# Half-sample fold, tables turned on TensorE, a given order on VectorE and ScalarE, and moved backward buffers in a spectral mixer with MLP

## Chip, cores, metric

One core of one Trainium2 chip. The metric is the device time of one execution in microseconds (us); a "run" is one execution, and a kernel's time is the median of its fast runs. A run more than 1.5% above the fastest of its kernel counts as slow; all comparisons below use the other, fast runs only, except where one slow run is shown as such. The granted clock is the share of its full clock that TensorE was given, as the profile reads it; "idle" is the time in which an engine is not busy.

## The reference

Sixteen-bit inputs and outputs, S = 2048 rows, D = 448 columns, F = 1792 hidden columns. The kernel computes the layer's output and the gradients of x, of the filter weights `w_r` and `w_i` (2048 x 225 each), and of the MLP's weights and biases.

```python
h  = x + irfft2(rfft2(layernorm(x)) * (w_r + 1j * w_i))      # over both axes
u  = gelu(einsum("bsd,sf->bdf", layernorm(h), w1) + b1)
h2 = h + transpose(einsum("bdf,fs->bds", u, w2) + b2)
# outputs: h2, and the vector-Jacobian product with grad_out for x, w_r, w_i, w1, b1, w2, b2
```

## The kernel before

The transforms are matmuls: a transform along the columns (tables `csF`), one along 16 row blocks (`Rm`), a re-sort through DMA, and a second transform (`Ut`, `Vt`), then the same backwards (`UTt`, `VTt`, `RTm`, `csI`). I call the stages: column transform, second transform, row inverse; the spectral part runs once forward (0 to about 138 us), then comes the MLP with the gradient of its hidden layer, then the spectral part again for the gradients. In between, "fill" matmuls of independent products (in the forward part the product of w2 and grad_out, later the gradients of w2 and w1) are put into TensorE's idle time by counts given by hand. The program's order is kept on TensorE and on the one DMA queue; VectorE and ScalarE are ordered by a scheduler.

```python
N_FILL_F = (50, 4, 16, 3, 16, 2)   # fill counts: ahead of the column transform, per tile in it,
                                   # ahead of the second transform, per step in it, after it, per row-inverse tile
tc.manual_schedule(engines={PE, SP})             # [arguments shortened]

def w_io(Wv, dr, di, store, eng):                # filter weights: 9 transfers for each of w_r, w_i
    for c_, d in ((0, dr), (1, di)):
        ...                                      # [cut] sb = Wv[part:P:8, g0:g1, c_, 0:DF]: rows of 225 numbers
        for f in range(4):
            go(f, 0, 16, ...); yield
            go(4 + f, g0, 16, ...); yield
        go(4, 0, 1, ...); yield

def w_mult(c2, xc, Wv, conj):                    # product with the weights: four VectorE operations,
    ...                                          # [cut] then one negation on ScalarE
    sc.activation(out=y[:, :, 2, :], in_=y[:, :, 0, :], func=ACT.Copy, scale=-1.0)

def bwd_mult(c2, xc):                            # in the loop of the backward second transform
    xs = Xs[:, 2 * c2:2 * c2 + 2, :, :]
    y = w_mult(c2, xc, W_view_B, True)
    ve.tensor_tensor(out=xs, in0=xs, in1=srow[...], op=ALU.mult)     # scale the stored coefficients
    ...                                          # [cut] four more VectorE operations: gradient of the weights

m448 = ring(r448, 0, 8, D)                       # eight row buffers
def load_xt(t):                                  # last stage: x comes back tile by tile
    xt = m448.next()
    nc.sync.dma_start(out=xt, in_=x_pt[:, t, :])
    xts.append(xt)
def gx_consumer(t, py):                          # five row buffers a tile: xt, gx, and three in ln_bwd
    xt = xts.pop(0)
    if t + 1 < NT: load_xt(t + 1)
    ...                                          # [cut] normalise, layer norm backward, store gx
```

## Time and profile before

Time before: 465.3 us (median of four runs, 464.8 to 469.7).

The head of the page of the kernel before: the span, each engine's busy time, the DMA packets, and the shares of the chain that ended last.

```profile
span 463.0 us, 6021 instructions
...
PE 370.3 (80%) x1920; PEld 187.3 (40%) x1920; DVE 261.9 (57%) x725; ACT 239.7 (52%) x485; POOL 51.8 (11%) x54
...
DMA packets 175144, 84.18 MB, mean 182 GB/s; under 512 B 123272, under 2 KB 170376, under 8 KB 174984
...
PE 44%; DVE 18%; DMA 18%; SPq 8%; ACT 6%; POOL 3%; issue 2%; DVEq 0%; ACTq 0%; POOLq 0%
```

No engine is busy throughout, so the time is made of waits between engines. Windows of the same kernel, for the forward part, the MLP, and the last two stretches of the backward part (the loop of the second transform with the weight product; then the row inverse, the gradient of w1 and the tail). Columns: window, its length, busy time of PE, PEld, DVE, ACT, POOL, then granted TensorE clock, DMA share, GB/s.

```profile
0.00:138.00 138.00, 95.83 (x506) 49.32 (x507) 105.13 (x330) 71.56 (x135) 48.77 (x50) 0.95 0.69 158
138.00:286.00 148.00, 136.18 (x723) 70.62 (x723) 87.27 (x226) 54.76 (x118) 2.73 (x3) 0.99 0.88 214
...
318.60:386.20 67.60, 56.38 (x262) 26.10 (x261) 30.72 (x64) 45.75 (x89) 0.00 (x0) 0.92 0.56 169
386.20:463.00 76.80, 55.31 (x313) 29.21 (x311) 35.22 (x97) 48.99 (x110) 0.00 (x0) 0.87 0.59 167
```

Read the first line so: TensorE works 95.8 of 138 us. TensorE's longest waits in the kernel before (sum, number of times, longest):

```profile
PE ps_ff L151 <- ACT rS L592: 15.1, 4, 8.6
PE ps_ff L151 <- DMA rX<-rX: 12.7, 6, 4.5
PE ps_mm L151 <- DMA rS<-in_B_w_dram: 10.0, 5, 3.0
...
PE ps_mm L151 <- DMA rst<-rE: 5.2, 1, 5.2
```

The first hides the weights: ScalarE's negation waits for VectorE's product, and that waits for the weight loads. The second is the transposes of x by DMA. And in the last stretch of the kernel before (386 us to the end), this is VectorE's largest wait by sum:

```profile
DVE r_80 L909 <- DMA out_dram<-r_80: 20.8, 14, 3.6
```

`r_80` is the ring of eight row buffers; VectorE waits for a store to free one.

### The profile page before, as it was taken

What the parts mean: (1) busy time and instruction counts of PE and PEld (TensorE: products, weight loads), DVE (VectorE), ACT (ScalarE), POOL (GpSimd) and SP (SyncE); (2) the same over time, 40 slices, a digit from 0 to 9 for tenths busy, and PEclk for the clock granted to TensorE, in tenths of its full rate; (3) what the DMA queues carried; (4) which work ended last, traced back from release to release, by engine and by line L of the source; (5) the groups of instructions that cost most, each with busy time, mean ns of one, the idle gap of its engine ahead of it and who ended that gap; (6) DMA issues with size and microseconds to landing.
All of it is one profiled execution on the core that took longest, in us unless ns stands there. A gap on an engine that the chain in (4) does not pass through costs nothing.

```text
span 463.0 us, 6021 instructions
## 1 busy us (share of the span) xinstructions
PE 370.3 (80%) x1920; PEld 187.3 (40%) x1920; DVE 261.9 (57%) x725; ACT 239.7 (52%) x485; POOL 51.8 (11%) x54
## 2 busy tenths in 40 slices
PE   2856577598979999788799999959389799898680
PEld 1323333244634545344355555424134355443340
DVE  9998952493892888621159777010186631443555
ACT  0646553375655564121223436735368677777671
POOL 6107996000000000000200000000000000000000
PEclk9989998799998999999999999988989899998885
DMA  8998897425325995699979995996645557667543
GB/s 254 238 205 154 172 148 179 110 80 144 119 121 162 328 303 129 148 280 227 289 145 228 181 207 89 197 225 200 170 154 175 159 164 215 177 163 196 160 149 130
DMA packets 175144, 84.18 MB, mean 182 GB/s; under 512 B 123272, under 2 KB 170376, under 8 KB 174984
## 3 DMA queue, kind: packets, MB, share of 16 engines
q1 hardware_dynamic: 175112, 83.80, 72.5%
q8 instruction: 15, 0.25, 0.2%
q14 instruction: 17, 0.14, 0.1%
HBM read 27.55 MB, written 22.04 MB: 107 GB/s over the span
## 4 chain that ended last, share of the span: by engine, by line
PE 44%; DVE 18%; DMA 18%; SPq 8%; ACT 6%; POOL 3%; issue 2%; DVEq 0%; ACTq 0%; POOLq 0%
PE ps_mm L151 36%; PE ps_ff L151 8%; SPq L489 5%; DMA out_dram<-r_80 5%; DMA r_80<-h_d 4%; DVE stats L644 3%; POOL Ut L403 2%; DVE r_80 L911 2%; DMA r_80<-in_A_x_dram 2%; DMA r_72<-in_B_w_dram 1%; DMA rst<-rE 1%; DMA rS<-in_B_w_dram 1%; DVE r_73 L298 1%; DMA rst<-rB 1%; DVE rB L682 1%
## 5 line engine op out<-in xcount | busy, mean ns | idle before, releaser
L151 PEld LDWEIGHTS <-rst 112*128 112x128 bf16 x480 | 47.4, 101 | 68.7 <-issue 11.4
L151 PE MATMUL ps_mm<-rC,rst 112*128 112x512 bf16 (+1 forms) x256 | 56.3, 367 | 10.9 <-DMA rst<-rB 8.7
L151 PE MATMUL ps_mm<-rG,rst 112*128 112x512 bf16 x224 | 55.1, 396 | 5.2 <-DMA rst<-rE 5.2
L151 PE MATMUL ps_mm<-rE,rS 128*128 128x448 bf16 x224 | 43.4, 353 | 10.0 <-DMA rS<-in_B_w_dram 10.0
L151 PE MATMUL ps_mm<-rB,r_72 128*128 128x448 bf16 x224 | 45.4, 362 | 3.4 <-DVE rB L757 2.2
L151 PE MATMUL ps_mm<-rC,rE 128*128 128x448 bf16 x144 | 37.7, 399 | 9.8 <-DMA rC<-in_grad_out_dram 8.9
L151 PEld LDWEIGHTS <-r_73 128*128 128x128 bf16 (+1 forms) x352 | 33.9, 111 | 27.6 <-issue 3.5
L151 PE MATMUL ps_mm<-rD,r_73 128*128 128x448 bf16 x224 | 43.3, 352 | 0.0
L151 PEld LDWEIGHTS <-rS 128*128 128x128 bf16 (+1 forms) x288 | 27.7, 98 | 35.3 <-DMA rS<-in_B_w_dram 12.2
L995 ACT CAST rO<-ps_mm 128x512 bf16<-128x512 f32 x56 | 32.4, 591 | 17.3 <-PE ps_mm L151 15.3
L1010 ACT CAST rO<-ps_mm 128x512 bf16<-128x512 f32 (+1 forms) x63 | 31.6, 536 | 6.0 <-PE ps_mm L151 4.7
L151 PEld LDWEIGHTS <-r_72 128*128 128x128 bf16 x224 | 22.3, 100 | 26.3 <-issue 6.5
L151 PE MATMUL ps_ff<-csI,rAT 113*128 113x448 bf16 x128 | 31.0, 367 | 1.8 <-ACT rAT L613 1.8
L865 DVE SCALAR_TENSOR_TENSOR r_80<-ps_mm,b2col,r_80 128x448 bf16<-128x448 f32 x16 | 10.8, 683 | 33.3 <-DMA r_80<-h_d 19.1
L872 ACT ACTIVATE r_80<-rC 128x448 bf16<-128x448 bf16 x16 | 9.2, 576 | 39.0 <-DMA out_dram<-r_80 35.7
L151 PEld LDWEIGHTS <-rE 128*128 128x128 bf16 x144 | 15.4, 107 | 29.6 <-issue 12.2
L905 ACT ACTIVATE r_80<-ps_mm 128x448 bf16<-128x448 f32 x16 | 8.7, 545 | 33.2 <-PE ps_mm L151 33.2
L151 PE MATMUL ps_ff<-rS,UTt 128*128 128x452 bf16 x32 | 12.1, 379 | 15.1 <-ACT rS L592 15.1
L613 ACT CAST rAT<-ps_ff 113x512 bf16<-113x512 f32 x32 | 18.5, 590 | 8.4 <-PE ps_ff L151 8.4
L906 DVE CUSTOM_DVE_ANT_0 r_80<-r_80 128x448 bf16<-128x448 bf16 x16 | 10.0, 624 | 22.6 <-ACT r_80 L905 15.4
L151 PE MATMUL ps_mm<-rC,rO 128*128 128x448 bf16 x80 | 20.5, 380 | 1.1 <-DMA rO<-in_B_w_dram 1.1
L586 DVE TENSOR_TENSOR rS<-rS,rD 128x904 bf16<-128x904 bf16 x8 | 5.0, 630 | 28.1 <-DMA rD<-in_A_w_i_dram 16.9
(198 smaller groups left out, 613.8 us busy)
## 6 DMA issues: line engine op xcount, KB each, us to landing
r_72<-in_B_w_dram SPq DMA_DIRECT2D x7, 1024.0 KB
rS<-in_B_w_dram SPq DMA_DIRECT2D x8, 896.0 KB
out_dram<-rO SPq DMA_DIRECT2D x14, 512.0 KB
out_dram<-rO SPq DMA_DIRECT2D x16, 448.0 KB
r_72<-r_77 SPq DMA_DIRECT2D x32, 113.0 KB
r_73<-r_77 SPq DMA_DIRECT2D x32, 113.0 KB
out_dram<-r_80 SPq DMA_DIRECT2D x32, 112.0 KB
rA<-in_A_x_dram SPq DMA_DIRECT2D x4, 448.0 KB
```

The lines of the kernel that those rows point to most:

```text
L151: nc.tensor.matmul(out, lhsT=lhsT, rhs=rhs, start=start, stop=stop)
L403: gp_.tensor_scalar(out=d[:, :, j], in0=comp, scalar1=msk[:, j:j + 1], scalar2=None, op0=ALU.mult)
L489: eng.dma_start(out=sb, in_=d_ap)
L613: sc.copy(out=aT[0:KC].rearrange("p a b -> p (a b)"), in_=pa[0:KC, :])
L644: ve.bn_stats(out=stats[:, t, :], in_=src[:, t, :])
L865: ve.scalar_tensor_tensor(out=h2, in0=py[:, 0:D], scalar=b2col[:, t:t + 1], in1=ht, op0=ALU.add, op1=ALU.add)
L872: sc.activation(out=junk, in_=go_pt[:, t, :], func=ACT.Copy, accum_out=gb2[:, t:t + 1])
L905: sc.activation(out=pb, in_=ps, func=ACT.Identity, scale=1.0, accum_out=ms)
L906: ve.tensor_tensor_reduce(out=w(junk), in0=w(pb), in1=nrm, scale=m2scale, scalar=0.0, op0=ALU.mult, op1=ALU.add, accum_out=m2)
L911: ve.scalar_tensor_tensor(out=out, in0=pb, scalar=rstd, in1=resid, op0=ALU.mult, op1=ALU.add)
L995: evac(out=o[:, c * 512:(c + 1) * 512], in_=pw[:])
L1010: evac(out=o[:, c * 512:c * 512 + n * P], in_=pw[:, 0:n * P])
```

## The change

Its intent: shorten the start by folding x about half samples (no separate first column, no normalised copy; the mean and the scale are applied later), transposing on TensorE instead of by DMA, and turning the inverse tables on TensorE instead of generating them; give VectorE and ScalarE an order by hand and share evacuations (the copies of matmul results out of TensorE's accumulator) between them by a load count; and in the backward part load the weights earlier into another buffer, with 8 instead of 18 transfers, turn du later, and bring x back in four loads outside the row buffers. The core of the diff, with cuts marked:

```diff
-N_FILL_F = (50, 4, 16, 3, 16, 2)
-N_FILL_B = (16, 16, 60, 9, 16, 12)
+ML_F = 4
+N_FILL_F = (12, 3, 20, 3, 24, 2)
+N_FILL_B = (16, 16, 40, 8, 32, 12)
@@ order and evacuations
-    ctx.enter_context(tc.manual_schedule(engines={mybir.EngineType.PE, mybir.EngineType.SP}))
+    ctx.enter_context(tc.manual_schedule(engines={mybir.EngineType.PE, mybir.EngineType.SP, mybir.EngineType.DVE,
+                                                  mybir.EngineType.Activation}))
-    evac = nc.any.tensor_copy
+    def evac(out, in_):
+        if load[0] <= load[1]:
+            sc.copy(out=out, in_=in_)
+        else:
+            ve.tensor_copy(out=out, in_=in_)
@@ weights [cut]
+            for p0, p1, g0, g1, row, dims in ((0, 64, 0, 16, 0, [[16 * DF, 4], [1, 16 * DF]]),
+                                              (64, 112, 0, 16, 112, [[-DF, 48], [1, DF]]),
+                                              (112, 128, 1, 16, 127, [[-DF, 15], [1, DF]]),
+                                              (112, 128, 0, 1, 64, [[1, DF]])):
@@ inverse tables, made inside the loop of the second transform [cut: about 90 lines of generated tables removed]
+    def gen_inv_s(h):
+        for i in range(4):
+            mm(pt[:, i * P:(i + 1) * P], lhsT=src[:, g0 + i, :], rhs=permI[:], start=True, stop=True)
+        evac(out=dst[:, g0:g0 + 4, :].rearrange("p g c -> p (g c)"), in_=pt[:])
@@ memset
-    gp_.memset(rB[:, NT * D:], 0.0)
+    gp_.memset(rB[:], 0.0)
@@ forward weights: transposes of w2 held back between the loads of w_r and w_i
-        for _ in range(6):
+        for _ in range(2 if c2 else 4):
             next(w_loads, None)
+        hold[0] = False
+        while held_w2:
+            held_w2.pop(0)()
@@ row inverse of the forward part
+        if s1 % 4 == 1 and s1 > 1:
+            rstd_of_h(s1 // 4 - 1)
+        if s1 >= 5:
+            norm_h(s1 - 5)
@@ last stage
-        xt = xts.pop(0)
-        if t + 1 < NT:
-            load_xt(t + 1)
+        xt = xall[:, t, :]          # xall: the buffer of the forward coefficients, filled by four loads
```

## The prediction

> **What bounds the kernel now.** No one engine: by the page, TensorE is busy 80% of 463.0 us, VectorE 57%, ScalarE 52%. The chain of waits is 44% TensorE, 18% DMA, 18% VectorE, 8% the DMA queue's issue. Windows by stage: spectral forward 0-138 us (TensorE busy 95.8, VectorE 105.1), MLP 138-286 (TensorE 136.2), spectral backward with both weight gradients 286-463 (TensorE 138.3, VectorE 69.5, ScalarE 113.4, clock 0.89).
>
> In the last stage TensorE's timeline names the waits: 5.2 us at 307 (operand transpose queued behind du's transposes), 8.6 at 328 (18 weight loads, 12.6 us of queue, only after du has left their buffer), 2.6, 2.1 and 4.0 for operand transposes behind small transfers, 1.7 for an evacuation, and a 13 us tail in which each tile waits for its store to free a row buffer. Of 119 weight-gradient evacuations here ScalarE does all but one.
>
> **What the change does.**
> - Forward: removes 16 normalisations (0.43 us each), the generated inverse tables (about 20 us of VectorE, 13 of GpSimd) and the GpSimd mask products (about 20 us); adds 16 masked copies on VectorE and ScalarE (estimate 0.4 us each), 105 small matmuls. VectorE's 105 us falls to about 97 by counting its new instruction order; x transposes leave the DMA queue (12.7 us of TensorE waits).
> - Weights: 18 issues per load become 8 (12.3 us of queue to about 5, estimate).
> - Backward: weights load before du is turned, into another buffer; du is turned after the forward half; x comes in four loads instead of sixteen, outside the row buffers, so the tail should run at VectorE's pace (about 2.2 us a tile, not 3.3); evacuations are split between two engines.
> - TensorE grows by 21,632 columns, 9.0 us at 2.4 GHz, mostly inside present idle time.
>
> **Stage estimates.** Forward 138 to 130: the column transform starts at about 20 instead of 30, but VectorE stays the limit (97 us, fixed order) and the forward tables end late, so the second transform starts near 66 instead of 73. One 8192-column GpSimd memset holds the gain down: in the trace two 226-column VectorE operations took 2.57 and 2.95 us beside GpSimd memsets, against 0.38 for 452 columns later; the Trainium skill, "GPSIMD Engine Reference", section "Key points", says the two engines share SBUF interfaces, and this agrees. I expect the first VectorE table operations to be held until about 12 us. MLP: 148, unchanged (DMA share 0.86-0.89, and TensorE). Backward 177 to 148: TensorE's work there is about 128 us at full clock; VectorE's 5.2 us per step against TensorE's 4.9 limits the weight product loop; the 22 us of named DMA waits go, the tail shrinks to about 8, and less idling keeps the clock up.
>
> **Prediction: 427 us, 8 in 10 between 411 and 443.** Faster by over 2%: 0.93; within 2%: 0.04; slower: 0.03.
>
> **What would show it.** Right: no TensorE wait over 2 us on weights or du after 286; VectorE over 85% busy in the forward; evacuations about even between engines; VectorE held by the memset near 3-12 us; MLP within 1.5 us. Wrong: TensorE waiting over 4 us for the masked tables before the second transform; long VectorE waits at the head of its fixed order; operand transposes still late behind stores.
>
> **What would make it wrong.** A hand-given order that blocks: an early instruction waiting for a DMA stops everything behind it. Or both evacuating engines saturating in the backward loops.

## The result

The changed kernel ("after") takes 447.7 us (median of four runs, 446.7 to 449.1). Its ratio to the kernel before is 0.960, with a 95% interval of 0.954 to 0.967. A ratio here is the mean time of one kernel's fast runs over that of the other's of the same rounds, so it is not quite the ratio of the medians that I quote. It is faster, by 18 us and not by the 38 predicted, and outside the range of 411 to 443.

The page and the windows of after, to be read beside those of before:

```profile
span 444.9 us, 6199 instructions
...
PE 374.7 (84%) x2089; PEld 195.2 (44%) x2089; DVE 295.7 (66%) x720; ACT 214.8 (48%) x435; POOL 13.4 (3%) x35
...
DMA packets 156040, 79.99 MB, mean 180 GB/s; under 512 B 105704, under 2 KB 150760, under 8 KB 155880
...
PE 42%; DMA 24%; DVE 22%; ACT 5%; issue 4%; SPq 2%; DVEq 0%; POOL 0%; ACTq 0%; POOLq 0%
```

```profile
0.00:140.00 140.00, 99.88 (x602) 55.07 (x603) 91.98 (x245) 74.90 (x144) 12.80 (x31) 0.96 0.66 134
140.00:288.00 148.00, 137.24 (x770) 72.33 (x768) 93.44 (x231) 56.29 (x116) 0.34 (x3) 1.00 0.84 207
...
320.10:381.10 61.00, 56.95 (x256) 25.38 (x256) 47.67 (x97) 32.65 (x66) 0.00 (x0) 0.94 0.68 194
381.10:444.90 63.80, 55.08 (x333) 30.15 (x331) 48.64 (x123) 39.23 (x89) 0.00 (x0) 0.98 0.83 215
```

The forward part did not get shorter: TensorE idles 140.0 - 99.9 = 40.1 us in it instead of 42.2, and works 4 us more. The MLP is the same. The backward loop (the second transform with the weight product) gained 6.6 us and the last stretch 13.0. TensorE's waits in after:

```profile
...
PE ps_mm L197 <- DMA rst<-rE: 6.2, 3, 4.8
PE ps_ff L197 <- ACT VTt L68: 5.4, 1, 5.4
PE ps_ff L197 <- ACT rO L68: 5.4, 1, 5.4
PE ps_ff L197 <- ACT rX L68: 5.3, 1, 5.3
```

The transposes of x (12.7) are gone, and three single waits for ScalarE of 5.3 to 5.4 us have come in the forward part. The first of the three in this list is a chain that the timeline of after shows. Columns: start, length, engine, what, number, and in brackets the idle time before it and what ended it.

```profile
52.91 2.68 SPq L513 DMA_DIRECT2D rG<-in_A_w_r_dram  x4
55.69 10.67 SPq L274 DMA_TRANSPOSE rE<-in_B_w_dram  x2
66.46 2.60 SPq L513 DMA_DIRECT2D rG<-in_A_w_i_dram  x4
...
```

```profile
77.83 1.17 DVE L68 TENSOR_TENSOR rS<-rX,rG 128x904 bf16<-128x904 bf16 x2 [5.23 <-DMA rG<-in_A_w_i_dram]
...
79.89 0.58 ACT L68 ACTIVATE rS<-rS 128x452 bf16<-128x452 bf16 x1 [6.65 <-DVE rS L68]
...
80.38 0.57 ACT L68 CAST VTt<-ps_ff 128x512 bf16<-128x512 f32 x1
...
81.00 0.59 PE L197 MATMUL ps_ff<-permI,Vt 128*128 128x128 bf16 x4 [5.41 <-ACT VTt L68]
```

The four loads of `w_i` leave the queue behind two transposes of w2 that hold it from 55.7 to 66.4 us. VectorE's product waits for them, ScalarE's negation waits for the product, and an evacuation that TensorE needs stands behind the negation in ScalarE's given order.

Where each stage begins on TensorE, from its timeline (us; f3 and p2 are experiments below):

| | before | after | f3 | p2 |
|---|---|---|---|---|
| first column transform | 30.1 | 21.3 | 15.4 | 26.1 |
| first second transform | 72.8 | 61.0 | 56.4 | 63.3 |
| first row inverse | 114.4 | 113.4 | 106.4 | 111.9 |
| last matmul of the MLP's first product | 181.4 | 185.3 | 179.7 | 184.5 |
| last matmul of the hidden gradient | 284.5 | 286.0 | 282.4 | 285.7 |
| backward second transform | 318.6 | 320.1 | 316.8 | 321.0 |
| last row inverse | 386.2 | 381.1 | 377.0 | 380.9 |
| end | 463.0 | 444.9 | 442.4 | 445.1 |

So after has a lead of 11.8 us at the second transform, 1.0 at the row inverse, and is 3.9 us behind at the end of the MLP's first product.

### The profile page after: what moved, and what is told of

Its sections match the earlier page's. It is cut to its first block, busy times and chain, and to the rows that moved or that the text cites. A ratio compares the mean times of both kernels' runs of the same rounds, so it can differ in the third digit from the quotient of the medians.

```text
span 444.9 us, 6199 instructions
## 1 busy us (share of the span) xinstructions
PE 374.7 (84%) x2089; PEld 195.2 (44%) x2089; DVE 295.7 (66%) x720; ACT 214.8 (48%) x435; POOL 13.4 (3%) x35
## 4 chain that ended last, share of the span: by engine, by line
PE 42%; DMA 24%; DVE 22%; ACT 5%; issue 4%; SPq 2%; DVEq 0%; POOL 0%; ACTq 0%; POOLq 0%
PE ps_mm L197 32%; PE ps_ff L197 8%; DVE rS L68 6%; DMA r_80<-h_d 4%; DMA rst<-rE 4%; DMA r_72<-in_B_w_dram 3%; DVE stats L68 3%; DMA rS<-in_B_w_dram 3%; DMA out_dram<-r_80 3%; DVE r_80 L68 2%; DMA out_dram<-rO 2%; DVE ident L68 2%; DMA rG<-in_A_w_i_dram 2%; DVE r_73 L68 2%; DVE rX L68 1%
## 5 line engine op out<-in xcount | busy, mean ns | idle before, releaser
L197 PE MATMUL ps_mm<-r_72,rst 112*128 112x512 bf16 (+1 forms) x256 | 54.8, 364 | 6.4 <-DVE rO L68 3.1
L68 ACT CAST rO<-ps_mm 128x512 bf16<-128x512 f32 (+1 forms) x69 | 38.4, 571 | 43.3 <-PE ps_mm L197 35.4
L68 DVE CAST rO<-ps_mm 128x512 bf16<-128x512 f32 (+1 forms) x51 | 32.2, 644 | 26.6 <-PE ps_mm L197 25.5
L197 PE MATMUL ps_mm<-rC,rE 128*128 128x448 bf16 x144 | 39.5, 395 | 8.7 <-DMA rC<-in_grad_out_dram 8.7
L197 PE MATMUL ps_mm<-rB,r_72 128*128 128x448 bf16 x224 | 43.2, 353 | 2.1 <-DMA r_72<-in_B_w_dram 2.0
L68 ACT CAST r_77<-ps_ff 128x452 bf16<-128x452 f32 x60 | 31.4, 547 | 3.7 <-PE ps_ff L197 3.6
L197 PE MATMUL ps_ff<-csI,rAT 113*128 113x448 bf16 x128 | 29.6, 353 | 3.4 <-DVE mvh L68 2.0
L68 ACT ACTIVATE rS<-rS 128x452 bf16<-128x452 bf16 x16 | 9.3, 581 | 31.4 <-DVE rS L68 31.2
L68 DVE BATCH_NORM_STATS2 stats<-rA 128x6 f32<-128x448 bf16 x32 | 19.9, 623 | 0.5
L197 PEld LDWEIGHTS <-rAT 113*128 113x128 bf16 x128 | 12.2, 98 | 16.1 <-ACT rAT L68 5.1
## 6 DMA issues: line engine op xcount, KB each, us to landing
out_dram<-rO SPq DMA_DIRECT2D x16, 448.0 KB
rA<-in_A_x_dram SPq DMA_DIRECT2D x4, 448.0 KB
```

The source lines that it names most:

```text
L68: fn(**kw)
L197: nc.tensor.matmul(out, lhsT=lhsT, rhs=rhs, start=start, stop=stop)
```

## The experiments

Eighteen kernels were run, each against the kernel before on the same chip, with six runs each. The table gives all; labels as in the text. Medians and ratios are of the fast runs: one run of c1 and of b1 and two of f5 and of f6 were slow and are left out. One run is a plain repeat of after (c1): 448.0 us and 0.964 from five fast runs (448.3 with the slow one), which I use as the reference for the rest, beside the 447.7 us and 0.960 of the first four runs of after. Lines of the kernel are numbered anew in each kernel; in after and its variants all operations of VectorE and ScalarE bear the line of one helper, so go by the tiles.

| run | edit | us | ratio to before | 95% |
|---|---|---|---|---|
| c1 | after, unedited | 448.0 | 0.964 | 0.959-0.968 |
| f1 | 18 weight transfers again | 453.1 | 0.970 | 0.967-0.974 |
| f2 | w_i loads ahead of w2 transposes | 451.4 | 0.966 | 0.963-0.970 |
| f3 | memset of pad columns only | 443.7 | 0.950 | 0.947-0.954 |
| f4 | f2 and f3 | 444.6 | 0.952 | 0.949-0.956 |
| f5 | f3, weights on GpSimd's queue | 460.4 | 0.989 | 0.985-0.993 |
| f6 | f3, last w2 transposes held | 443.8 | 0.950 | 0.945-0.955 |
| s1 | scheduler's order on VectorE, ScalarE | 442.3 | 0.952 | 0.948-0.956 |
| s2 | scheduler's order in the last part only | 441.2 | 0.948 | 0.944-0.952 |
| b1 | no backward weight loads (wrong result) | 441.1 | 0.946 | 0.942-0.950 |
| b2 | backward weights from a packed copy | 441.9 | 0.949 | 0.945-0.953 |
| b3 | scale multiplications out of the loop | 443.7 | 0.953 | 0.950-0.957 |
| p1 | more fill in idle slots | 449.5 | 0.968 | 0.963-0.972 |
| p2 | fill counts as before | 446.7 | 0.959 | 0.955-0.963 |
| q1 | kernel before, x in four loads | 450.9 | 0.963 | 0.958-0.968 |
| v1 | f3, b2 and s2 together | 427.9 | 0.921 | 0.917-0.925 |
| v2 | f3, b2 and b3 together | 430.3 | 0.924 | 0.919-0.929 |
| v3 | v1, normalisation two tiles later | 426.0 | 0.912 | 0.908-0.917 |

### Forward: are the weights late, and does it matter? (f1, f2, f3, f4)

f1, the 18 transfers again (the two large transfers of each part split by f):

```diff
-            (0, 64, 0, 16, 0, [[16 * DF, 4], [1, 16 * DF]]), (64, 112, 0, 16, 112, [[-DF, 48], [1, DF]]), ...
+            four of slice(f, 64, 4) and three of slice(64 + f, 112, 3), same rows; the rest as it was
```

> Edit: the kernel after, with each part of the filter weights again loaded by nine transfers instead of four (same bytes, same pieces of 450 bytes, same places in the order), forward and backward. The prediction held that eighteen issues on the queue cost 12.3 us and eight about 5 us, and that this is most of the weights' lateness. Theory A (issue count): each stage's weights land about 7 us later, so the whole is 6 to 12 us slower than after, about 455 us. Rival B (the data movement of the short rows and the queue order set the landing; the issues only fill time in which the queue waits anyhow): within 2 us of after, 446 to 450 us.

It took 453.1 us: 5.2 us more than c1 by the medians, 0.7% or 3 us by the ratios to before, whose intervals overlap. That lies between the two theories, below A's 6 to 12 us and above B's 2. In its profile the MLP's first product begins at 143.2 us, 3.2 later than in after, and the forward wait behind the weights (`VTt`) is 7.7 us instead of 5.4; the backward stretch with the other weight loads is no longer than in after (shown below with b2). The number of transfers costs something in the forward part, and less than the prediction counted.

f2, the order of the queue:

```diff
-        for _ in range(2 if c2 else 4):
+        for _ in range(8):
             next(w_loads, None)
```

> Edit: the kernel after, with the four loads of the imaginary filter weights issued right after the four of the real ones in the forward transform, ahead of the held transposes of w2. Theory A (queue order): in the profile of after they left the queue at 66.5 to 69.1, behind two transposes that took it from 55.7 to 66.4, and landed near 77.8, which held VectorE 5.2 us, ScalarE behind it 6.7 us and TensorE 5.4 us. With the edit they land before 70 us, the 5.4 us wait at 75.6 is gone, and the start of the MLP (139.2 us in after) comes 4 to 7 us earlier: 441 to 444 us. Rival B: the waits only move, since the w2 transposes then land later and the fill products or the last D3 writes wait for them: within 2 us of after.

Theory A fell. TensorE's 5.4 us wait for `VTt` is gone, and this stands in its place among its waits:

```profile
PE ps_mm L197 <- DMA rE<-in_B_w_dram: 5.7, 1, 5.7
```

That is the fill product waiting for a transposed tile of w2, which now comes behind the weights. The MLP's first product began at 140.9 us in place of 140.0. One wait was swapped for another, as rival B said.

f3, the memset. In after, VectorE starts so (first GpSimd's memset, then VectorE):

```profile
3.64 6.92 POOL L736 MEMSET rB<- 128x8192 bf16 x1
```

```profile
1.59 9.30 DVE L68 TENSOR_SCALAR ident<-r_73,cols 128x128 bf16<-128x128 f32 x1 [1.59 <-POOL cols L333]
...
10.93 1.08 DVE L68 TENSOR_SCALAR r_73<-r_73,cols 128x226 f32<-128x226 f32 x4
```

```diff
-    gp_.memset(rB[:], 0.0)
+    gp_.memset(cut(rB, 0, NT, 4, P)[:, :, :, DC:P], 0.0)
```

> Edit: the kernel after, with GpSimd zeroing only the 1024 pad columns of the 8192-column buffer, since the rest is written before it is read. In after that memset took 6.92 us (3.64 to 10.56) and VectorE's first table work waited until 10.9 us. Theory A (the start limits the forward stage): VectorE is free by about 5 us, the column transform starts 5 to 6 us earlier (15.5 instead of 21.3 us) and all of it stays: 442 us. Rival B (the later weights and the queue order set the end of the forward stage): the transform starts earlier but the wait for the weights at 75 us grows by as much, and the whole gains 0 to 2 us: 446 to 448 us.

The same two VectorE lines of f3:

```profile
1.59 3.33 DVE L68 TENSOR_SCALAR ident<-r,cols 128x128 bf16<-128x128 f32 x1 [1.59 <-POOL cols L333]
...
4.96 1.08 DVE L68 TENSOR_SCALAR r<-r,cols 128x226 f32<-128x226 f32 x4
```

VectorE is free 6.0 us earlier, the column transform starts 5.9 us earlier, and the table of stages shows 5.6 us of it still there at the end of the MLP's first product. Theory A held, and the whole gained 4.3 us by medians. The Trainium skill, "GPSIMD Engine Reference", section "Key points", names the shared SBUF interfaces of GpSimd and VectorE; a VectorE operation that takes 3.33 us with short memsets beside it takes 9.30 us with a long one.

> Edit: both of the two before together. If the weights' landing is what eats the early start, the two together gain more than the sum of each alone: 434 to 440 us, the MLP starting at 128 to 132 us. If the forward stage is held by something further (VectorE's own 90 us of work in it, or the D3 writes behind the w2 transposes at 109 to 113 us), the two together gain no more than the larger of them alone: 441 to 444 us.

f4 took 444.6 us, no better than f3 alone: TensorE waited 3.5 us for the later w2 tile. Together with f2 this settles that putting `w_i` first is no gain.

### Which queue, or which pieces? (f5, b1, b2)

```diff
-                    nc.sync.dma_start(out=sb, in_=d_ap)
+                    gp_.dma_start(out=sb, in_=d_ap)
```

> Edit: only the pad columns zeroed, as in the third run, and all sixteen weight loads issued from GpSimd's queue instead of the one of SyncE; the forward ones may then leave as early as the buffer is free. Theory A (the queue's order is what makes the weights late, there is bandwidth to spare): no wait for weights anywhere in the forward stage, TensorE's wait at about 70 us gone, the MLP starts at 129 to 132 us against 134.4 in the third run, the backward stretch of 32 us loses 4 to 8 us, and the whole takes 430 to 437 us. Rival B (the short pieces themselves load the DMA engines, whichever queue carries them): the transposes of w2 and the operand transposes run as late as in the third run, and the whole is within 3 us of its 443.7 us.

f5 was 17 us slower than f3. The forward loads left as early as the buffer allowed and met the first loads: TensorE's waits for grad_out and for w2 grew to

```profile
PE ps_mm L197 <- DMA rC<-in_grad_out_dram: 17.3, 3, 8.5
PE ps_mm L197 <- DMA rE<-in_B_w_dram: 13.2, 1, 13.2
```

In the backward part the loads left earlier as well, all eight between 3.7 and 8.5 us into the stretch shown next (in after between 6.7 and 23.7 us), and the stretch was as long. The stretch from the last matmul of the hidden gradient to the backward second transform, in after, f5, b1 and b2 in this order:

```profile
286.00:320.10 34.10, 27.11 (x150) 13.45 (x149) 15.51 (x32) 13.74 (x25) 0.25 (x1) 0.95 1.03 152
```

```profile
299.40:333.50 34.10, 27.00 (x151) 13.69 (x149) 15.67 (x32) 13.88 (x26) 5.54 (x9) 0.90 0.98 170
```

```profile
286.90:312.60 25.70, 24.82 (x149) 13.24 (x147) 15.42 (x32) 13.84 (x26) 0.40 (x2) 1.00 0.52 153
```

```profile
288.50:314.30 25.80, 24.91 (x150) 13.32 (x149) 15.52 (x32) 13.91 (x26) 0.00 (x0) 1.00 0.86 217
```

f5 equals after to a tenth of a microsecond (so exact a match is luck: the granted clock was 0.90 and 0.95). The column before the last, the DMA engines' share, reads 1.03 in after and 0.98 in f5: they are busy throughout. The Trainium skill, "DMA: Bandwidth & Descriptors", section "Issuing engines are not separate DMA queues", says that transfers started by different engines run on the same 16 DMA engines; this agrees.

b1 leaves the backward loads out (its result is wrong):

```diff
-    for _ in range(3):
-        next(w_back, None)          # [both places, and the rest loop]
+    gp_.memset(rC[:, NT * D:NG * 2 * KW], 0.0)
```

> Edit: the kernel after, with the eight loads of the filter weights in the backward stage left out; the product then multiplies by what the buffer held before, so the first three and the gradient outputs that depend on it are wrong on purpose. After has 32 us from the last evacuation of the MLP's gradient to the first matmul of the backward second transform (288.0 to 320.1 us), where 23 us had been predicted. Theory A (the weights' data and their place in the one queue delay the operand transposes and the writes of the transposed rows): the wait of 4.8 us for an operand at 313 us goes, this stretch shrinks to 23 to 27 us, and the whole gains 5 to 9 us: 439 to 443 us. Rival B (the operand transposes and row writes are slow by themselves, or TensorE is slow there from its clock): the stretch stays above 29 us and the whole gains under 3 us.

The stretch fell to 25.7 us and the whole to 441.1. The loads cost 8.4 us there, and without them the DMA share is 0.52. Theory A held, but it joined two things, the data and the place in the queue. b2 separates them: the same bytes at the same places, in other pieces.

```diff
+    w_d = dram.tile([P, NG * 2 * KW], BF16, name="w_d")               # after the forward transforms
+    nc.sync.dma_start(out=w_d[:], in_=rG[:, 0:NG * 2 * KW])
-    w_back = w_io(W_view_B, A_w_r, A_w_i, False)
+    for q in range(4):                                                # [cut] one, one and two at the three former places
+        nc.sync.dma_start(out=rC[:, n * q:n * (q + 1)], in_=w_d[:, n * q:n * (q + 1)])
```

> Edit: the kernel after, with the filter weights of the backward stage read back from a packed copy: at the end of the forward transforms the arranged weights are written once to a scratch tensor (128 rows of 14.5 KB), and the backward stage reads them with four transfers of 128 pieces of 3.6 KB in place of eight made of 450-byte pieces. The bytes are the same. Theory A (the 450-byte pieces load the DMA engines, which is why another queue did not help): the stretch from the end of the MLP's gradient to the backward second transform, 34.1 us in after and 25.7 us without any weight loads, comes to 26 to 29 us, and the whole gains 4 to 8 us: 440 to 444 us. Rival B (the bytes or the issues count, not the pieces): the stretch stays above 32 us and the whole is within 2 us of after's 448.

25.8 us, as good as no loads at all, and 441.9 us in all. The packets of b2's page, beside those of after above:

```profile
DMA packets 152535, 81.84 MB, mean 186 GB/s; under 512 B 101560, under 2 KB 146616, under 8 KB 152248
```

There are 4144 packets fewer under 512 bytes, and 1.85 MB more in all, since the copy is also written once. The DMA share in the stretch fell from 1.03 to 0.86. The granted clock rose from 0.95 to 1.00 as the wait of 4.8 us went, and TensorE's busy time fell by 2.2 us with it. Theory A held: read in larger pieces, the same bytes cost the stretch nothing. The Trainium skill, "DMA: Bandwidth & Descriptors", section "Specifications", gives 512 bytes as the least transfer for line rate; these pieces lie just under it, and this agrees, though no run here tries a size between 450 bytes and 3.6 KB. b2 also has fewer transfers (4 for 8). That is not what helped: f1 has 18 of them in the same stretch, with the same pieces as after, and it is no longer (the line of f1):

```profile
291.50:325.50 34.00, 28.25 (x150) 13.90 (x148) 15.50 (x32) 13.74 (x25) 0.25 (x1) 0.90 0.98 152
```

One thing stays unexplained: on GpSimd's queue, in f5, the profile counts these loads as 608 packets for 1.84 MB, 3.0 KB each on the mean, and the stretch is as long. So it is the layout in rows of 450 bytes that costs, and the count of packets in the profile does not tell how.

### The given order (s1, s2, b3)

```diff
-    engines={PE, SP, DVE, Activation}
+    engines={PE, SP}
```

> Edit: the kernel after, with VectorE and ScalarE again ordered by the scheduler, as before the change; TensorE and the DMA queue keep the order of the program. Theory A (the given order pays): the scheduler's order pulls work forward that blocks evacuations, 450 to 460 us. Rival B (the given order is where the forward gain went, since ScalarE waited 6.7 us for VectorE's weight product with TensorE's evacuation behind it): the wait of 5.4 us at 75.6 us shrinks to under 3 us and the whole takes 440 to 446 us.

s1 was 6 us faster than after, but not where rival B put it. Its forward part was 4.7 us longer (the MLP's first product began at 144.7), so the given order pays there. It was shorter from the end of the hidden gradient on. Its backward loop, with the same instructions on the same engines:

```profile
322.60:377.90 55.30, 53.15 (x258) 24.68 (x257) 44.39 (x91) 33.94 (x66) 0.00 (x0) 1.00 0.76 207
```

against 61.0 us in after, and VectorE has 91 instructions in it where after has 97. The scheduler had pulled work out of the loop. The line of after's loop where VectorE limits, a stretch of 30 us, reads VectorE busy 29.2 of 30 (TensorE reads 29.5 in it, so this line alone does not decide between the two; b3 below does):

```profile
330.00:360.00 30.00, 29.45 (x138) 13.20 (x137) 29.21 (x60) 17.60 (x37) 0.00 (x0) 1.00 0.54 162
```

> Edit: the kernel after, with VectorE and ScalarE in the order of the program up to the second MLP stage, and ordered by the scheduler from the gradient of the hidden layer on. With the scheduler everywhere (442.3 us) the forward stage ended 4.7 us later than after's and everything after it took 8 us less. Theory A (the two effects are separate): this run keeps the forward's 140 us and gains the backward's 6 to 8 us: 438 to 442 us. Rival B (the scheduler gains by moving backward work of VectorE into the forward and MLP stages, which the split forbids): within 2 us of after, 446 to 450 us.

s2 took 441.2 us with the backward loop at 55.0 us. Theory A held for the backward part; the forward part kept only about half of its gain (142.6 us).

b3 keeps the given order and moves one thing (with the making of `srow`, the row of scales, before it):

```diff
-        ve.tensor_tensor(out=xs, in0=xs, in1=srow[...], op=ALU.mult)      # in bwd_mult
+        if t < 8:                                                          # in the hidden gradient's loop
+            xs = Xs[:, 2 * t:2 * t + 2, :, :]
+            ve.tensor_tensor(out=xs, in0=xs, in1=srow[...], op=ALU.mult)
```

> Edit: the kernel after, all in the order of the program, with the eight multiplications of the stored forward coefficients by the row of scales (0.63 us each, 5 us in all) taken out of the loop of the backward weight product and put into the first eight steps of the hidden layer's gradient, where VectorE waits for TensorE. Theory A (the hand-given order lost the backward gain by keeping this in the loop that VectorE limits): the stretch from the backward second transform to the last inverse transform, 61.0 us in after and 55.3 us with the scheduler's order, falls to 55 to 57 us, and the whole gains 4 to 6 us: 442 to 444 us. Rival B (the scheduler's gain lies elsewhere, in the order of evacuations): under 2 us gained.

```profile
320.40:376.40 56.00, 53.28 (x257) 24.50 (x257) 43.45 (x89) 32.49 (x65) 0.00 (x0) 1.00 0.67 192
```

The loop fell by 5.0 us to 56.0, and the whole by 4.3. The ten other profiles with after's loop have 59.2 to 61.3 us there, so at least 3 us of this is clear of their spread; the granted clock rose with it, from 0.94 to 1.00. Theory A held: the loop is VectorE's, and eight operations that could run anywhere earlier stood in it.

### The lead of the forward part (f6, p1, p2, v3)

f6 holds the last transposes of w2 until the writes of the second transform have left the queue.

```diff
+            if make_inv and c2 == nh + lag - 2:
+                hold[0] = True
         ...
         flush()
+        hold[0] = False
+        while held_w2:
+            held_w2.pop(0)()
```

> Edit: only the pad columns zeroed, as in the third run, and the last w2 transposes of the forward stage held back until the writes of the second transform have left the queue. In after the last two of those writes stood behind two w2 transposes (106.1 to 110.9 us) and TensorE waited 3.2 us; in the third run 3.6 us. Theory A (queue order): that wait goes and the MLP starts 2 to 4 us earlier than the third run's 134.4 us, the whole near 441 us. Rival B (the held transposes then arrive late for the fill products, which wait instead): within 1 us of the third run, 443 to 445 us.

443.8 us from its four fast runs (445.5 over all six), no better than f3, and the MLP's first product began at 136.7 us, 2.3 us later than in f3: rival B. TensorE waited 5.0 us for a tile of w2.

p1 and p2 change only fill counts.

```diff
-N_FILL_F = (12, 3, 20, 3, 24, 2)
+N_FILL_F = (30, 3, 28, 3, 24, 0)     # p1
+N_FILL_F = (50, 4, 16, 3, 16, 2)     # p2
```

> Edit: the kernel after, with only the counts of fill matmuls changed: 30 instead of 12 ahead of the column transform and 28 instead of 20 ahead of the second transform, taken from the last stretch of the forward stage (the row inverse has none). TensorE idles 5.3 us at 16 to 21 us and 5.4 us at 55 to 61 us in after, waiting for ScalarE. Theory A (what counts is TensorE's idle time; the early start was bought by moving fill work back): the fills drop into those two idle slots, the column transform starts within 1 us of 21.3, the row inverse shortens by 5 us, and the MLP starts 3 to 6 us before 140.0: 442 to 445 us. Rival B (later waits for weights and the queue set the end of the forward stage): the MLP starts at 140 within 1 us, 447 to 449 us.

p1 gave nothing: 449.5 us. The fills did drop into idle time (the column transform began at 21.5 us with 18 more of them ahead of it), but the row inverse, now without fills, did not get shorter; its first matmul came at 111.7 us and the MLP's at 142.6. That is 30.9 us for 26.6 in after, at a granted clock of 0.79 for 1.00. So theory A was right about the slots and wrong about the end: taking work from TensorE does not shorten this stretch.

> Edit: the kernel after, with the counts of fill matmuls in the forward stage as in the kernel before (50 ahead of the column transform, 4 a tile in it, 16 ahead of the second transform, 16 after it). Theory A (the start was bought with fill work): the column transform starts 4 to 9 us later, at 25 to 30 us, the row inverse is 5 to 7 us shorter, and the MLP starts within 3 us of 140.0: 445 to 451 us. Rival B (the early start is a real lead that other waits eat): the MLP starts 5 us or more later and the whole takes over 453 us.

p2 took 446.7 us. The column transform started 4.8 us later than in after, the row inverse began 1.5 us earlier, and the MLP's first product ended 0.8 us earlier. Rival B, which expected over 453 us, is refuted, and more than half of the earlier start of the column transform (4.8 of 8.8 us) was fill work put off. But the second transform still starts at 63.3 us, 9.5 us earlier than before, so most of the lead there is real and is lost later. Most of it is lost in the second transform, 48.6 us in p2 for 41.6 in the kernel before (before's line, then p2's), of which TensorE is busy 39.7 for 34.6:

```profile
72.80:114.40 41.60, 34.61 (x159) 16.43 (x158) 21.78 (x45) 23.17 (x46) 4.42 (x4) 0.88 0.46 113
```

```profile
63.30:111.90 48.60, 39.66 (x198) 19.63 (x196) 25.79 (x52) 23.33 (x55) 0.09 (x1) 0.85 0.74 125
```

The row inverse was not shorter either, 26.8 us from its first matmul to the MLP's first, against 26.6 in after.

v3 asks what paces that stretch. In v1, ScalarE waits there three times for VectorE's scale, with the evacuation that TensorE needs behind it. ScalarE's wait in v1 in this stretch (TensorE has 2.4 us behind the queue there at its start, and 3.2 us in three waits of about one, for the evacuations behind these scales):

```profile
ACT rB L68 <- DVE nmr_h L68: 3.7, 3, 1.8
```

```diff
-        if s1 >= 5:
-            norm_h(s1 - 5)
+        if s1 >= 7:
+            norm_h(s1 - 7)
```

> Edit: the fastest kernel so far (427.9 us, v1), with the normalisation of each tile of h standing seven tiles behind its row inverse instead of five, so that ScalarE does not meet it before VectorE has made the scale. In v1 ScalarE waited 0.6, 1.4 and 1.8 us there and TensorE 3.7 us in the 26.7 us of the row inverse. Theory A (this head-of-order wait paces the stretch): it shrinks to 23 to 25 us and the whole is 424.5 to 426.5 us. Rival B (the later normalisations only delay the first matmuls of the MLP, which need them): the same within 1.5 us, or slower.

In v3 ScalarE has no such wait, TensorE only the 2.4 us at the start, and the stretch is 22.8 us instead of 26.7 (v1's line, then v3's):

```profile
106.10:132.80 26.70, 23.31 (x165) 13.62 (x166) 20.86 (x52) 18.22 (x32) 0.00 (x0) 1.00 0.53 162
```

```profile
106.30:129.10 22.80, 22.72 (x165) 13.76 (x166) 20.18 (x52) 17.25 (x30) 0.00 (x0) 1.00 0.62 189
```

The MLP's first product ended 2.9 us earlier (175.1 for 178.0). Theory A held: a head-of-order wait on ScalarE, which the given order had brought, paced the row inverse. The whole gained 1.9 us by the medians, with intervals of the ratio that just touch; the same three waits of ScalarE, 3.7 us, are in after's profile.

### What the gain was made of (q1)

q1 makes one part of the change in the kernel before.

```diff
-        xt = xts.pop(0)
-        if t + 1 < NT:
-            load_xt(t + 1)
+        xt = xall[:, t, :]      # four loads into the buffer of the forward coefficients, ahead of the loop
```

> Edit: the kernel before, with one part of the change alone: x comes back in four loads into the buffer of the forward coefficients for the last layer norm, instead of sixteen loads into the row buffers. Theory A (as predicted, each tile waited for its store to free a row buffer, and that cost the tail): the stretch from the last row inverse to the end, 76.8 us in before and 63.8 in after, falls to 66 to 71 us, the part after the last matmul from 13 to 8 us or less, and the whole gains 5 to 10 us: 455 to 460 us. Rival B (ScalarE's evacuations and the operand transposes pace that stretch, and the tail only follows them): under 3 us gained, 462 us or more; then the 13 us that after gained there came from sharing the evacuations.

450.9 us, ratio 0.963, the same as the whole change (0.960 and 0.964). Its last stretch, and VectorE's wait for a row buffer in it:

```profile
387.50:449.80 62.30, 51.22 (x313) 28.14 (x311) 36.92 (x102) 47.73 (x106) 0.00 (x0) 0.98 0.73 206
```

```profile
DVE r L911 <- DMA out_dram<-r: 7.7, 4, 3.2
```

76.8 us fell to 62.3, more than theory A asked for; after has 63.8 there with its evacuations shared by two engines. ScalarE alone, with 47.7 us of work in 62.3, was no limit. So no gain from sharing the evacuations shows in that stretch, though no run takes the sharing alone out of after.

### Do the causes add up? (v1, v2, c1)

> Edit: three edits together: only the pad columns zeroed, packed weights for the backward stage, and VectorE and ScalarE in the scheduler's order from the hidden layer's gradient on. Each alone against after's 448.3: about -4.5, -6.3 and -7.1 us. If they are separate causes, they add up: 430 to 433 us, with the MLP starting near 136 us, 26 us before the backward second transform and 55 to 56 us in it. If two of them remove the same wait, 435 us or more.

> Edit: the same as the run before it but with the order of the program everywhere and the eight scale multiplications moved ahead of the loop. Each alone: -4.5, -6.3 and -4.6 us. If they add up: 432 to 435 us. If the scheduler's order gave only what moving the multiplications gives, this run and the one before it agree within 1.5 us.

Off the ratio of c1, f3 is 0.0133, b2 0.0146, s2 0.0158 and b3 0.0104 lower. The first three sum to 0.964 - 0.0437 = 0.920, and v1 measured 0.921; the first two and b3 to 0.925, and v2 measured 0.924. The causes are separate. (In microseconds both came out 2 us below the ranges expected, which were counted from another chip's 448.3.) v1 and v2 differ by 2.4 us in the median, with intervals that overlap, so most of what the scheduler's order gave is the moved multiplications.

> The kernel after, unedited: a control on the chip of the other runs of this group, since the second MLP stage (the one that reads w2 and h) took 51.7 us in the profile of after and 53.7 to 55.4 us in the profiles of the four edits before, none of which touches it. If the chips differ in how fast they fetch, this run shows 53 to 55 us there and 448 to 451 us in all; if the edits did it, 51.7 and 447.7 us.

c1's timed runs agree with after, and with both of its theories, and its profile can't decide. The other profiles do: the second MLP stage, which the edits do not touch, took 53.5 to 55.3 us on the chip of f1 to f4, 51.6 to 52.1 on that of s1, b1 and f5, and 55.5 in q1 for 53.2 in before. So it differs with the chip or the run, by up to 4 us. c1's profiled execution was one of a kind and is used for nothing else: 645.5 us, with this row of the granted clock in tenths.

```profile
PEclk9755555555555555555555555555555555555555
```

The fastest kernel, v3, takes 426.0 us, ratio 0.912 to the kernel before, 5% below after's.

## Why the prediction was wrong

The direction was right, the size was not: 38 us predicted, 18 measured.

- **Forward, 138 to 130: wrong, 140.** The step that failed is the one behind "the second transform starts near 66 instead of 73" and "forward 138 to 130": I took the earlier start as a gain and let the rest of the part stay as long as it was (72.8 to 138 us before, so 65 us). The second transform started even earlier than predicted, at 61.0, and the rest took 79 us, 14 more. I had not asked where the fill work went: before the second transform stood 50 + 16 x 4 + 16 = 130 fill matmuls, and in after 12 + 16 x 3 + 20 = 80. But this is the smaller part: p2, with the 130 again, takes 75.4 us from there to the MLP, so 10 us of the 14 are in the stretch itself. Some three of these are in the row inverse (26.8 us in p2 for 23.6), where v3 removed a wait at the head of ScalarE's given order and gained 3.9; I had named such waits only as a general risk. The other seven are in the second transform, 48.6 us in p2 for 41.6. There TensorE's busy time grew by five and its idle time by two (lines at p2 above), and the table turns, 40 matmuls inside this stretch, are 4.4 us of the five. So "TensorE grows by 21,632 columns, mostly inside present idle time" failed here: the turns were put into a stretch whose length grew with them.
- **"VectorE stays the limit (97 us)": wrong.** VectorE was busy 92.0 of 140 us, 66%, not over 85%.
- **The memset: right.** I said VectorE would be held until about 12 us; its first free table operation came at 10.93. I took this as given; f3 shows it was worth 4 to 6 us to remove (by the medians and by the ratios).
- **Weights, "12.3 us of queue to about 5": right for the queue, wrong for what it is worth.** The two times four forward loads took 2.68 + 2.60 us of the queue. In the forward part they still landed near 77.8 us, behind transposes of w2, and in the backward part their pieces of 450 bytes made the stretch with the operand transposes and row writes 8.3 us longer, whatever the queue and the number of transfers (b1, b2, f5, f1). "The 22 us of named DMA waits go" failed here: the weight wait itself went, and 6.2 us of waits for operands stayed, one of 4.8. This is close to the sign that I had named for being wrong, late operand transposes; I had put them behind stores, and they were late beside the weight loads.
- **Backward, 177 to 148: mis-sized, 157.** Most of the missing 9 us is these weights: in b2 the part from the last matmul of the hidden gradient to the end takes 152.3 us, in after 158.9. The loop's mechanism was right: VectorE, 97% busy, at 5.5 us a step where I had counted 5.2. That five of its 61 us need not be there (b3) I had not seen. With less idling the granted clock did rise, from 0.89 to 0.96.
- **The tail: right in kind, too small.** I gave the tail five microseconds, 13 to 8; from TensorE's last matmul to the end it fell from 13.2 us to 5.3, and the last stretch gained another five ahead of that. The x loads alone shortened the last stretch by 14.5 us (q1), and the whole by 17 by the medians of that chip (468.2 and 450.9), which is as much as the whole change. If it is worth as much in after as alone, the rest nets to nothing within the intervals: the backward loop gained 6.6 us and the forward part up to the end of the MLP's first product lost 3.9.
- **Evacuations about even: right (69 and 51 on ScalarE and VectorE); no use of it shows in the last stretch (q1).**
- **MLP unchanged: right, 148 and 148.**

What stays open: of the 79 us that the forward part takes from the second transform on, about 10 more than in the kernel before remain even with its fill counts (p2: 75.4 us up to the MLP's first matmul; before: 65.2 us up to the steady stream of them, at 138). The row inverse explains three to four. The rest lies in the second transform; it has the table turns inside it (4.4 us of TensorE), one step more of lag, a wait for a table of 3.7 us and one of 2.8 behind the queue (before it had waits too, of 6.4 and 4.2 us). No run takes the turns out of it, and f2, f4 and f6 each shortened one of these waits and got another in its place, so I can't give each its share.

## What to carry to other kernels

An earlier start is a gain only if it is still there at the end of the stage: before costing it, add up each engine's work and idle time over the whole stage, ask where the filling work went, and what new work does to the part that it is put into. When an engine gets a hand-given order, look for operations that wait for another engine's result and stand ahead of an evacuation, and for work in the limiting loop that could stand anywhere earlier. And a many-part change should be taken apart in the kernel before as well as in the kernel after: one part, x in four loads, gained as much in the kernel before as the whole change did.

## What the Trainium skill lacked or had wrong

- "DMA: Bandwidth & Descriptors", section "Specifications", has the limit of 512 bytes but not what pieces just below it do to other transfers: with the same 1.84 MB, pieces of 450 bytes instead of 3.6 KB lengthened a stretch of 25.8 us to 34.1, in which operand transposes and small writes run beside them (after and b2).
- "TensorE: Matmul & The Clock Gate", Part 1, tells of half clock after idle time, and the trace agrees (after the 4.84 us wait at 313 us, 16 matmuls took 5.31 us, 0.33 each, where others of that form take about 0.22; the granted clock reads 0.50 from 313.5 to 316.5 us). It has nothing that I could match to the one execution of c1, with a clock of 1.00 in its first 20 us, of 0.56 from 30 us on, and of 0.572 on the mean of its 645.5 us, with a busy TensorE.
